# Two blocks of 384 tokens, not 256, in steps of seven products, with the outer products of the last 256 tokens put off to the end

## The chip, the core and the metric

The kernel runs on one core of one Trainium2 chip. The metric is the device time of one execution in microseconds. TensorE (PE) has a queue for its matmuls; its weight loads (PEld) overlap them. VectorE is DVE, ScalarE is ACT, GpSimd is POOL, and SP issues the DMAs. Every engine takes its instructions in the order in which the kernel wrote them.

## What is computed

```python
scores = scale * q @ k.T                      # B, H, S, D = 4, 8, 576, 64, causal
local = softmax(scores) @ v
q_p = phi(q)                                  # phi(x) = max(x, 0) + min(exp(x), 1)
mem_out = (q_p @ M_prev) / (q_p @ z_prev + 1e-6)
x = g * mem_out + (1 - g) * local             # as 2304 tokens x 512
out = ((x @ w_a) * (x @ w_b)) @ w_out         # 512 -> 1536 -> 512
```

## The kernel before

All large products are made of float32 operands split into a high and a low part (float32r), as three matmuls: high by high, low by high, high by low. The first 207 us are attention, with the results (`xo`) stored to DRAM (`xs`). Then comes the gated MLP on tokens as columns. The 1536 hidden features are 12 tiles `f` of 128.

**Columns.** Tokens are taken in blocks `t`: 0 to 3 of 384 tokens, 4 of 256. One pair (t, f) is called a column, and columns are numbered: block 2 is 24 to 35, block 3 is 36 to 47, block 4 is 48 to 59. A column is, on PE, 12 matmuls for `a` and 12 for `b` (`half`, L923, as wide as the block), and then the outer products of the column before it (`outer`, L961: 3 matmuls of 128x512 for each 128 tokens, which add into a PSUM bank each). Beside it ACT copies `b` (L936), DVE multiplies it by `a` (L939, "mx"), ACT rounds the result to the high part (L943) and DVE subtracts for the low part (`split_lo`, L201, tile `hl`). The third matmul of the outer products reads `hl`.

**Memory units.** The memory term of a block is made in units (block t, rows j) while PE works on earlier columns. `plan` says behind which column each part of a unit is written: on DVE `phi2`, `norm`, `norm2` (L1092 to L1126, the "first half"), then `norm3`, `turn`, `turn_l` (L1131 to L1137 and L201, the "turn", which waits in the middle for an ACT pass `yh`), then `join` (L1164); `sums` (L1147) on POOL adds the two halves of `xs` that `x_load` has fetched; `retrieve` (L1157) is PE's part.

**Steps.** The last 512 tokens, two blocks of 256, are taken together in 12 steps `step7(f)`. Sums and differences of the blocks (`combine`, L1192; `split_x`, L1205) and of the weight tile's quarters (`sums_load`, L1226, `sums_of` on POOL, L1236, `sums_split`, L1249 and L201) replace 8 half products by 7 (`part`, L1270, 6 matmuls each). Four products end in `h` (DVE L1309, L1310) and `u`; the outer products of a step (`out_rows`, L1342, 12 matmuls of 128x512) follow in the next step. PSUM has 8 banks: 4 hold the products (`ab`, `ab2`, two each), 4 the sums of the outer products (`o0` to `o2`, `m`). The bank of a step's first product is that of the step before, and is free once that step's `h` (L1310) has read it:

```python
        al = bank("ab")
        part(al, a11, B11, True)
```

The last 768 tokens thus take 24 + 42 matmuls of width 256 for each f, and 18 of width 512.

`ws` holds the weights of the 12 tiles as plain float32 in DRAM. `attention` opens PSUM pools `ps_t` (six banks) and `ps_w` (two, for the attention output `pw`), which are closed before `ab`, `o`, `o1` are opened over the same banks.

Of the kernel before, what the change touches and what calls it, by code (L numbers as in the profile page):

```python
# [136 lines left out]
def kernel(  # L137
# [37 lines left out]
    TH = 256  # L175
# [190 lines left out]
    def attention(late, early, tiles, after, more, beyond):  # L366
# [586 lines left out]
    def outer(t, f, h, ms=None):  # L953
        wh, wl = wt[f]
        w0 = 2 * KK * P
        for m in ms or range(WIDTH[t] // P):
            if f == 0:
                key = "o1" if t == 1 else "o"
                po[t, m] = pools[key].tile([P, DM], F32, tag=f"{key}{m}", name=f"{key}{m}")
            for n, (hx, w) in enumerate(((h[0], wh), (h[0], wl), (h[1], wh))):  # L960
                nc.tensor.matmul(  # L961
                    po[t, m], lhsT=hx[:, m * P:(m + 1) * P], rhs=w[:, w0:w0 + DM],
                    start=(f == 0 and n == 0), stop=(f == NFT - 1 and n == 2),
                )

    def written(t, m):
        if t == 2:
            ob = xf[0][:, (0, 3, 2)[m]].rearrange("p k c -> p (k c)")
        elif t == NB:
            ob = xf[0][:, m].rearrange("p k c -> p (k c)")  # L970
        elif t == 3:
            ob = pools["mem_b"].tile([P, DM], F32, tag=("q4", "ph", "q4")[m], name="ob", bufs=(2, 1, 2)[m])
# [7 lines left out]
        nc.sync.dma_start(out=out[r0:r0 + P, :], in_=ob)  # L980

# [6 lines left out]
    def hidden(c, n):  # L988
# [15 lines left out]
    def column(c, between):  # L1004
# [7 lines left out]
        if f == NFT - 1:  # L1012
            for m in range(WIDTH[t] // P):
# [10 lines left out]
    def memory_unit(pool, ps_m, t, j):  # L1024


        J = 1 if t < NB - 1 else 2
        js = slice(j, j + J)
        T0, TW = START[t], WIDTH[t]
# [37 lines left out]
        def x_load():  # L1067
            if J == 1:
# [7 lines left out]
            else:  # L1076
                x = xf[0][:, 3]
                if (t, j) == rest[-1]:
                    x = pool.tile([P, J, TW], F32, tag="q4", name="xx", bufs=2)
                r["x"] = xf[0][:, (1 + j + t - NB) % 4], x  # L1080
# [104 lines left out]
    PLACE = {B22: 0, B11: 1, T1: 1, TT2: 1, T4: 1, B12: 2, T3: 2, B21: 3}  # L1185
# [52 lines left out]
    def sums_split(f):  # L1238
# [4 lines left out]
        if f % 3 == 2:  # L1243
            two = [w[:, 0:3 * Q] for w in wt[0]]
        else:
            two = [pools["ring"].tile([P, 3 * Q], F32R, tag=f"s{f % 3}{n}", name="s" + n) for n in "hl"]
        ring[f] = two, [w[:, 2 * Q:3 * Q] for w in wt[f]]
# [4 lines left out]
    def step7(f):  # L1252
# [6 lines left out]
        a11, a12, a22 = (quarter(wt[f], i) for i in (0, 1, 3))  # L1259
# [33 lines left out]
        else:  # L1293
            split_x(T4, B22)
            sums_load(3)
# [7 lines left out]
        if f:  # L1303
            sums_split(f + 1)
            sums_load(f + 3)
# [7 lines left out]
        def hh(i, h):  # L1313
            two[i] = [pools["w2"].tile([P, TB], F32R, tag=nm, name=nm)[:, 0:TH] for nm in ("hh", "hl")]
            nc.scalar.activation(out=two[i][0], in_=h, func=AF.Copy)

        def hl(i, h):
            split_lo(nc.vector, two[i][1], h, two[i][0])

        hh(0, h1)  # L1320
        if f < NFT - 1:
            prev[4]()
        hl(0, h1)
        sums_of(f + 2)
        part(ga, s4, B22)
        if f == NFT - 1:
            prev[4]()
# [5 lines left out]
        def out_rows(i):  # L1333
            wh, wl = (w[:, 4 * Q:4 * Q + DM] for w in wt[f])
            for m in (2 * i, 2 * i + 1):
                if f == 0:
                    key, tag = (("o", "o2"), ("m", "m"), ("o", "o0"), ("o", "o1"))[m]
                    po[NB, m] = pools[key].tile([P, DM], F32, tag=tag, name=tag)
                a = (m - 2 * i) * P
                hi, lo = (x[:, a:a + P] for x in two[i])  # L1340
# [10 lines left out]
    def last_rows(m):  # L1351
        t, f = columns[-1]
        outer(t, f, cols[len(columns) - 1][1][1:], (m,))
        written(t, m)

    def arrange(c):
        at = c - 4 * NFT
        if at == 0:
            pieces()
            split_x(B11)  # L1360
        if at == 1:
            combine(T1)
            split_x(T1)
        if at == 2:
            combine(TT2)
            split_x(TT2)
        if at == 3:
            combine(T3)
        if at == 4:
            split_x(B21)  # L1370
            combine(T4)
        if at == 5:
            memb.close()
            md.close()
            for key, n in ("xe", 1), ("ring", 1), ("u", 1), ("ob", 2):
                pool(mlp_r, key, "right", n)
            xc[T3] = [
                pools["xe"].tile([P, 2, TH], F32R, name=f"xe{n}") for n in "hl"
            ]
            split_x(T3)  # L1380
            sums_load(0)
        if at == 6:
            sums_of(0)
        if at == 7:
            sums_split(0)
            sums_load(1)
        if at == 8:
            sums_of(1)
        if at == 9:
            sums_split(1)  # L1390
            sums_load(2)
# [3 lines left out]
    columns += [(t, f) for t in range(2, NB) for f in range(NFT)]  # L1395
# [8 lines left out]
    for j in range(KK):  # L1404
        c = 2 * NFT + (0, 3, 6, 8)[j]
        planned(3, j, (c - 1, False, 0, 2), (c, False, 2, 11), (c + 2, True, 11, 15))
    AT = range(36, 48, 2)
    rest = (4, 0), (4, 2), (5, 0), (6, 0), (6, 2), (5, 2)
    for n, (t, j) in enumerate(rest):
        c = AT[n]  # L1410
        for o, mid, what in (
            (-3 if n else -2, True, "load"), (-1 if n else 0, False, "phi phi2 norm norm2"),
            (0, False, "x_load"), (0, False, "norm3 turn turn_h turn_l"), (1, False, "sums"),
            (2, True, "retrieve join"), (2, False, "join_h join_l" if t < NB else ""),
        ):
            plan.setdefault((c + o, mid), []).extend((t, j, nm) for nm in what.split())

    def unit_step(t, j, nm):
# [5 lines left out]
        if nm == "load":  # L1424
            if t == NB - 1 and j == 0:
# [3 lines left out]
                xf[0] = pools["xf"].tile([P, 4, 2, TH], F32, name="xf")  # L1429
# [10 lines left out]
    with tc.manual_schedule():  # L1440
# [85 lines left out]
        last["h"] = None, None, None, lambda: last_rows(0), lambda: last_rows(1)  # L1526
        for f in range(NFT):
            step7(f)
        for go in last["h"]:
            go()  # L1530
# [32 lines left out]
```

## Time and profile before

| | us |
|---|---|
| median of 3 runs (665.22 to 666.14) | 665.34 |
| the profiled execution | 666.34 |
| its span, first to last instruction | 664.2 |
| PE busy in the span | 652.4 |
| DVE busy in the span | 499.0 |

The granted TensorE clock is full (1.00) from the start to 650 us, and 0.94 on average in the last 14 us. A matmul's time in the trace is longer than the distance to the next one, since matmuls are pipelined; what PE takes for one is therefore read from the starts of successive matmuls.

### The profile page before, as it was taken

Reading aid. Unit: us, or ns where it says so; the run is one execution under the profiler, and the core shown is the slowest. Engines: PE = TensorE matmul, PEld = TensorE weight load, DVE = VectorE, ACT = ScalarE, POOL = GpSimd, SP = SyncE. Lnnn points to the kernel's source line nnn. Section 1 sums busy time; section 2 is a strip of 40 time slices with the busy share of each in tenths; the row PEclk is TensorE's granted clock in tenths of the full one; section 3 lists DMA queues with packets and bytes.
Section 4 is the critical chain, followed back from the end, with each engine's and each line's share of the span. In section 5 each row is a group of like instructions: output and inputs, shape, how many; then the busy total and the mean of one; then the engine's idle time right before and its main releaser. Section 6 shows DMA issues by size and latency. Waiting matters only on the chain.

```text
span 664.2 us, 12217 instructions
## 1 busy us (share of the span) xinstructions
PE 652.4 (98%) x4338; PEld 600.9 (90%) x4338; DVE 499.0 (75%) x1012; ACT 333.2 (50%) x797; POOL 273.4 (41%) x400
## 2 busy tenths in 40 slices
PE   9899999999989999999999999999999999999997
PEld 7788899999978999999999999999999999999996
DVE  6999998888888887879898757458766433666664
ACT  6999999999885544544323222222222323332221
POOL 4999999999993222124102201000100012344410
PEclk9999999999999999999999999999999999999999
DMA  8965657466833444533345432133220111211101
GB/s 182 198 183 132 161 127 192 116 180 180 264 117 136 160 153 163 183 123 72 100 139 163 150 113 69 20 100 71 70 57 25 47 33 64 96 65 64 64 33 63
DMA packets 131259, 76.88 MB, mean 116 GB/s; under 512 B 98816, under 2 KB 118272, under 8 KB 131200
## 3 DMA queue, kind: packets, MB, share of 16 engines
q1 hardware_dynamic: 131200, 76.12, 40.6%
q8 instruction: 34, 0.56, 0.4%
q14 instruction: 25, 0.20, 0.1%
HBM read 55.64 MB, written 20.45 MB: 115 GB/s over the span
## 4 chain that ended last, share of the span: by engine, by line
PE 81%; DVE 8%; SPq 3%; ACT 3%; DMA 2%; POOL 1%; issue 1%; ACTq 0%; DVEq 0%; POOLq 0%
PE pp L923 32%; PE o L961 16%; PE pp L1270 9%; PE pt L197 6%; PE pw L711 5%; PE pt L545 4%; PE o L1342 4%; DVE PT L201 3%; DVE nm L584 2%; SPq L1053 2%; POOL P L611 1%; PE m L1157 1%; PE m L1342 1%; PE pw L545 1%; ACT P L594 1%; DMA qr<-in_q_dram 1%
## 5 line engine op out<-in xcount | busy, mean ns | idle before, releaser
L923 PE MATMUL pp<-xh,wh 128*128 128x384 f32 (+1 forms) x472 | 153.7, 326 | 1.5 <-ACT xo L720 0.8
L923 PE MATMUL pp<-xh,wl 128*128 128x384 f32 (+1 forms) x472 | 153.5, 325 | 0.0
L923 PE MATMUL pp<-xl,wh 128*128 128x384 f32 (+1 forms) x472 | 153.2, 325 | 0.0
L923 PEld LDWEIGHTS pp<-xh,wh 128*128 128x128 f32 x472 | 88.9, 188 | 4.5 <-ACT x L936 1.2
L923 PEld LDWEIGHTS pp<-xl,wh 128*128 128x128 f32 x472 | 88.9, 188 | 2.4
L923 PEld LDWEIGHTS pp<-xh,wl 128*128 128x128 f32 x472 | 88.9, 188 | 0.0
L611 POOL TENSOR_SCALAR P<-P,sum 128x384 f32<-128x384 f32 (+4 forms) x144 | 80.8, 582 | 4.9 <-DVE sum L603 4.5
L936 ACT ACTIVATE x<-pp 128x384 f32<-128x384 f32 (+1 forms) x59 | 27.5, 467 | 102.0 <-PE pp L923 86.7
L1236 POOL TENSOR_TENSOR xf<-xf 128x256 f32<-128x256 f32 x48 | 36.3, 757 | 99.7 <-DMA xf<-ws 55.3
L201 DVE TENSOR_TENSOR PT<-pt,PT 128x512 fp32r<-128x512 f32 (+2 forms) x112 | 62.7, 588 | 10.4 <-ACT PT L666 8.1
L594 ACT ACTIVATE P<-pt,nm 128x128 f32<-128x128 f32 (+3 forms) x128 | 66.8, 530 | 5.1 <-DVE nm L584 3.4
L939 DVE TENSOR_TENSOR x<-pp,x 128x384 f32<-128x384 f32 (+1 forms) x59 | 31.1, 527 | 48.2 <-ACT x L936 46.1
L961 PE MATMUL o<-wh,hl 128*128 128x512 f32 x168 | 66.3, 395 | 0.0
L961 PE MATMUL o<-wl,hh 128*128 128x512 f32 x168 | 66.3, 394 | 0.0
L961 PE MATMUL o<-wh,hh 128*128 128x512 f32 x168 | 66.2, 394 | 0.0
L711 PE MATMUL pw<-PT,vh 128*128 128x320 f32 (+4 forms) x416 | 63.0, 295 | 1.0 <-DVE PT L201 0.6
L711 PEld LDWEIGHTS pw<-PT,vh 128*128 128x128 f32 x416 | 57.6, 189 | 3.6 <-DVE PT L201 1.9
L584 DVE TENSOR_REDUCE nm<-pt 128x1 f32<-128x128 f32 (+3 forms) x128 | 55.8, 478 | 3.5 <-PE pt L545 3.2
L866 POOL TENSOR_SCALAR wt<-wt 128x512 f32<-128x512 f32 (+1 forms) x21 | 21.0, 1000 | 83.8 <-ACT wt L860 83.8
L197 PE MATMUL pt<-ident,P 128*128 128x128 f32 (+1 forms) x400 | 52.8, 276 | 2.5 <-POOL P L611 1.0
L666 ACT ACTIVATE PT<-pt 128x512 fp32r<-128x512 f32 (+2 forms) x112 | 52.6, 526 | 2.8 <-PE pw L711 1.7
L943 ACT ACTIVATE hh<-x 128x384 fp32r<-128x384 f32 (+1 forms) x60 | 30.1, 501 | 40.6 <-DVE x L939 31.2
(192 smaller groups left out, 1471.6 us busy)
## 6 DMA issues: line engine op xcount, KB each, us to landing
xs<-xo SPq DMA_DIRECT2D x16, 576.0 KB, 4.6
xx<-xs SPq DMA_DIRECT2D x32, 192.0 KB, 3.5
wr<-in_moe_w_a_dram SPq DMA_DIRECT2D x12, 512.0 KB, 3.7
wr<-in_moe_w_b_dram SPq DMA_DIRECT2D x12, 512.0 KB, 4.8
wr<-in_moe_w_out_dram SPq DMA_DIRECT2D x12, 512.0 KB, 5.7
ws<-fw SPq DMA_DIRECT2D x24, 256.0 KB, 2.5
xf<-ws SPq DMA_DIRECT2D x12, 512.0 KB, 3.2
qr<-in_q_dram SPq DMA_DIRECT2D x34, 128.0 KB, 3.2
```

Of the source, the lines that this page charges most:

```text
L197: nc.tensor.transpose(out, x, ident[0:x.shape[0], 0:x.shape[0]])
L201: eng.tensor_tensor(out=lo, in0=x, in1=hi, op=ALU.subtract)
L545: nc.tensor.matmul(o, lhsT=w, rhs=x, start=first, stop=True, skip_group_check=True)
L584: nc.vector.tensor_reduce(out=s["nm"][:, c:c + 1], in_=src, axis=AX.X, op=ALU.min)
L594: nc.scalar.activation(out=s["P", i][:, h, :], in_=src, func=AF.Exp, scale=-1.0, bias=s["nm"][:, c:c + 1], accum_out=s["sums"][:, c, 0:1],)
L611: nc.gpsimd.tensor_scalar(out=pr[:, h, :], in0=pr[:, h, :], scalar1=r[:, c:c + 1], scalar2=1.0, op0=ALU.mult, op1=ALU.mult,)
L666: nc.scalar.activation(out=dst, in_=src, func=AF.Copy)
L711: nc.tensor.matmul(pv[:, a:hi], lhsT=w, rhs=x, start=(n == 0), stop=(n == len(ops) - 1))
L923: nc.tensor.matmul(pp, lhsT=w[:, w0:w0 + P], rhs=x[:, kk, :], start=(c == 0), stop=(c == 3 * KK - 1),)
L961: nc.tensor.matmul(po[t, m], lhsT=hx[:, m * P:(m + 1) * P], rhs=w[:, w0:w0 + DM], start=(f == 0 and n == 0), stop=(f == NFT - 1 and n == 2),)
L1236: nc.gpsimd.tensor_tensor(out=o, in0=x, in1=y, op=op)
L1270: nc.tensor.matmul(o, lhsT=a[:, kk * P:(kk + 1) * P], rhs=b[:, kk, :], start=first and c == 0, stop=True, skip_group_check=True,)
```

## The change

Blocks 4 and 5 are now both 384 wide and go through `step7` together; block 4 as a block of columns of its own is gone. For each f the last 768 tokens take 42 matmuls of width 384. The outer products of those tokens need six banks of sums and only four are there, so those of the last 256 tokens are put off: `h` of these tokens is kept for all 12 tiles in SBUF (`kept`), and `end` computes their outer products behind step 11, one group of 512 columns and two of 256, in the banks that the products have left. To make room, block 3 takes its tiles in the order 9, 10, 11, 0 to 8, the weights of the three are given up, and `back` makes parts of them again from `ws` in steps 7 to 9. The quarter sums have one buffer for odd and one for even tiles in place of three; `sums_split(f + 1)` now stands in step 0 too. Eight memory units 384 wide (4 for each of blocks 4 and 5) replace six units of two row groups 256 wide, and `TURN` sets their places in half columns. `ps_w` is opened before `ps_t`.

```diff
-    START = [0, TB, 2 * TB, 3 * TB, 4 * TB, 4 * TB + TH, 4 * TB + 2 * TH]
-    WIDTH = [TB] * 4 + [TH] * 3
-    NB = 5
+    NB = 4
+    START = [t * TB for t in range(NB + 2)]
...
+        ps_w = late.enter_context(tc.tile_pool(name="ps_w", bufs=1, space=bass.MemoryType.PSUM))
         ps_t = late.enter_context(tc.tile_pool(name="ps_t", bufs=1, space=bass.MemoryType.PSUM))
-        ps_w = late.enter_context(tc.tile_pool(name="ps_w", bufs=1, space=bass.MemoryType.PSUM))
...
+    ORDER = {t: list(range(NFT)) for t in range(NB)}
+    away = range(NFT - 3, NFT)
+    ORDER[NB - 1] = [*away, *range(NFT - len(away))]
...
+    def back(f):
+        if f in away:
+            for c in slice(0, 2 * Q), slice(3 * Q, 4 * Q):
+                hi, lo = (w[:, c] for w in blocks_of(f))
+                nc.scalar.activation(out=hi, in_=ring[f][:, c], func=AF.Copy)
+                split_lo(nc.vector, lo, ring[f][:, c], hi)
+
+    def kept(f):
+        if f < len(away):
+            return [w[:, 3 * Q:4 * Q] for w in wt[away[f]]]
+        return [w[:, 0:Q] for w in blocks_of(f)]
...
-        if f % 3 == 2:
-            two = [w[:, 0:3 * Q] for w in wt[0]]
+        if f % 2 == 0:
+            two = [w[:, 0:3 * Q] for w in wt[away[0]]]
...
             split_x(T4, B22)
-            sums_load(3)
...
-        if f:
-            sums_split(f + 1)
-            sums_load(f + 3)
+        sums_split(f + 1)
+        if f == 0:
+            sums_load(2)
+        sums_load(f + 3)
...
+        for g in range(len(rest)):
+            late_rows(g, *range(NFT - 1))
+        second()
+        for g, (o, a, c0, n) in enumerate(rest):
+            late_rows(g, NFT - 1)
+            leave(o[:, 0:n], *OUT[4 + g], START[NB] + 4 * P + a, g % 2, c0)
...
-        if at == 9:
-            sums_split(1)
-            sums_load(2)
+        if at == 11:
             sums_split(0)
             sums_load(1)
             sums_of(1)
...
-    AT = range(36, 48, 2)
+    TURN = [50, 53, 61, 63, 70, 73, 75, 78, 80, 83, 85, 88]
```

DVE's queue late in block 3, before: the multiplications (L939) of columns 46 and 47 with what stands ahead of and between them. `m` and `xf` belong to a unit's `join`, `ph`, `q` and `yl` to its turn.

```order
L1164 TENSOR_TENSOR xf<-m,xf 128x512
L939 TENSOR_TENSOR x<-pp,x 128x384
L201 TENSOR_TENSOR hl<-x,hh 128x384
L1131 TENSOR_TENSOR ph<-ph,n_6644 128x512
L1137 STREAM_TRANSPOSE q_6479<-ph 128x512
L201 TENSOR_TENSOR yl<-q_6479,yh 128x512
L939 TENSOR_TENSOR x<-pp,x 128x384
```

The same queue after the change, from column 43's multiplication (L937 now) to that of column 44; the rows of width 768 are `split_x` and `combine`.

```order
L937 TENSOR_TENSOR x<-pp,x 128x384
L200 TENSOR_TENSOR hl<-x,hh 128x384
L200 TENSOR_TENSOR wl_4553<-xf,wh_4552 128x768
L1205 TENSOR_TENSOR xf<-xf 128x768
L1171 TENSOR_TENSOR xf<-m,xf 128x384
L1138 TENSOR_TENSOR ph<-ph,n_6569 128x384
L1144 STREAM_TRANSPOSE q_6479<-ph 128x384
L200 TENSOR_TENSOR yl<-q_6479,yh 128x384
L937 TENSOR_TENSOR x<-pp,x 128x384
```

The sums of blocks that stood in the columns of block 4 now stand between the units in block 3.

DVE's queue at the passage from the columns to step 0, before: the last column's multiplication, then step 0 down to its `h`.

```order
L939 TENSOR_TENSOR x<-pp,x 128x256
L201 TENSOR_TENSOR hl<-x,hh 128x256
L1290 TENSOR_TENSOR u_7318<-pp,x 128x256
L201 TENSOR_TENSOR xl_83<-xf,xh_82 128x512 x2
L1301 TENSOR_TENSOR u_7344<-pp,x 128x256
L1302 TENSOR_TENSOR u_7344<-u_7344,pp 128x256
L1309 TENSOR_TENSOR h_7359<-pp,x 128x256
L1310 TENSOR_TENSOR h_7359<-pp,h_7359 128x256
```

After the change, the same place (`wl_4521` and `wl_3642` are `sums_split(0)`, `sl` and `wl_3775`'s low part `sums_split(1)`):

```order
L200 TENSOR_TENSOR hl<-x,hh 128x384
L200 TENSOR_TENSOR wl_4521<-xf,wh_4520 128x768
L200 TENSOR_TENSOR wl_3642<-xf,wh_3641 128x256
L1319 TENSOR_TENSOR u_6858<-pp,x 128x384
L200 TENSOR_TENSOR xl_85<-xf,xh_84 128x768 x2
L1329 TENSOR_TENSOR u_6883<-pp,x 128x384
L1330 TENSOR_TENSOR u_6883<-u_6883,pp 128x384
L200 TENSOR_TENSOR sl<-xf,sh 128x768
L200 TENSOR_TENSOR wl_3776<-xf,wh_3775 128x256
L976 COPY xf<-o_6144 128x512
L1338 TENSOR_TENSOR h_6910<-pp,x 128x384
L1339 TENSOR_TENSOR h_6910<-pp,h_6910 128x384
```

Both splits of quarter sums, which stood behind columns 55 and 57 of 60, moved to the passage itself, the second in front of `h`.

## Rows read from the trace of the kernel before

**Rows 1.** Profile page, part 1: busy us (share of the span) xinstructions of each engine.
```profile
PE 652.4 (98%) x4338; PEld 600.9 (90%) x4338; DVE 499.0 (75%) x1012; ACT 333.2 (50%) x797; POOL 273.4 (41%) x400
```
**Rows 2.** Windows: stretch, length, busy us (instructions) by engine, clock, DMA share, GB/s.
```profile
325.00:350.00 25.00, 25.00 (x134) 23.36 (x133) 22.81 (x53) 7.50 (x16) 2.30 (x2) 1.00 0.51 138
450.00:475.00 25.00, 25.00 (x138) 23.34 (x137) 19.34 (x44) 7.30 (x14) 3.01 (x2) 1.00 0.33 71
575.00:600.00 25.00, 25.00 (x172) 23.14 (x171) 16.47 (x36) 6.45 (x16) 9.07 (x13) 1.00 0.19 64
```
**Rows 3.** Waits of PE, 150 to 664 us: total us, times, longest.
```profile
PE pp L923 <- ACT xo L720: 0.8, 1, 0.8
```
**Rows 4.** Timeline, PE: start us, us, engine, line, operation.
```profile
416.76 0.39 PE L961 MATMUL o<-wh,hh 128*128 128x512 f32 x1
...
423.59 0.39 PE L961 MATMUL o<-wh,hh 128*128 128x512 f32 x1
...
559.42 0.40 PE L961 MATMUL o<-wh,hh 128*128 128x512 f32 x1
...
563.69 0.40 PE L961 MATMUL o<-wh,hh 128*128 128x512 f32 x1
```
**Rows 5.** Chain that ended last, two steps: start us, us, what xcount.
```profile
577.53 1.39 PE o L1342 x6
...
585.31 1.40 PE o L1342 x6
```
**Rows 6.** Timeline, DVE, 332 to 447 us: parts of units, one column's pair.
```profile
332.06 0.56 DVE L1095 SCALAR_TENSOR_TENSOR ph<-q,ph 128x384 f32<-128x384 f32 x1
...
335.30 0.56 DVE L1131 TENSOR_TENSOR ph<-ph,n 128x384 f32<-128x384 f32 x1
...
338.04 0.35 DVE L1092 TENSOR_SCALAR ph<-ph 128x384 f32<-128x384 f32 x1
...
436.93 0.56 DVE L939 TENSOR_TENSOR x<-pp,x 128x384 f32<-128x384 f32 x1 [4.63 <-ACT x L936]
438.08 0.56 DVE L201 TENSOR_TENSOR hl<-x,hh 128x384 fp32r<-128x384 f32 x1 [0.59 <-ACT hh L943]
438.56 0.68 DVE L976 COPY xf<-o 128x512 f32<-128x512 f32 x1
...
444.12 0.69 DVE L1131 TENSOR_TENSOR ph<-ph,n 128x512 f32<-128x512 f32 x1
...
446.86 0.55 DVE L939 TENSOR_TENSOR x<-pp,x 128x384 f32<-128x384 f32 x1
```
**Rows 7.** Timeline, one quarter split and one set of quarter sums.
```profile
557.75 0.84 ACT L1249 ACTIVATE sh<-xf 128x768 fp32r<-128x768 f32 x1 [1.09 <-POOL xf L1236]
...
558.62 0.96 DVE L201 TENSOR_TENSOR sl<-xf,sh 128x768 fp32r<-128x768 f32 x1 [1.50 <-ACT sh L1249]
...
563.30 3.25 POOL L1236 TENSOR_TENSOR xf<-xf 128x256 f32<-128x256 f32 x4 [5.59 <-DMA xf<-ws]
```
**Rows 8.** Profile page, part 6: DMA xcount, KB each, us to landing.
```profile
xf<-ws SPq DMA_DIRECT2D x12, 512.0 KB, 3.2
```
**Rows 9.** Timeline: a POOL addition and the DVE instruction beside it.
```profile
492.46 1.29 POOL L1147 TENSOR_TENSOR xf<-xf 128x512 f32<-128x512 f32 x1 [12.12 <-DMA xf<-xs]
...
492.84 1.32 DVE L201 TENSOR_TENSOR hl<-x,hh 128x384 fp32r<-128x384 f32 x1 [0.59 <-ACT hh L943]
```
**Rows 10.** Groups by form, DVE, 420 to 664 us: xcount | busy us, mean ns.
```profile
L201 DVE TENSOR_TENSOR hl<-x,hh 128x384 fp32r<-128x384 f32 x15 | 9.8, 654 | 8.9 <-ACT hh L943 8.9
```
**Rows 11.** Timeline, 206 to 214 us, and the last copy.
```profile
206.21 0.74 ACT L720 ACTIVATE xo<-pw,ungate 128x576 f32<-128x576 f32 x1 [0.69 <-PE pw L711]
207.00 0.45 PE L923 MATMUL pp<-xh,wh 128*128 128x384 f32 x1 [0.83 <-ACT xo L720]
...
213.35 0.55 DVE L939 TENSOR_TENSOR x<-pp,x 128x384 f32<-128x384 f32 x1
...
660.51 0.69 DVE L976 COPY xf<-o 128x512 f32<-128x512 f32 x1 [0.70 <-PE o L1342]
```

More of the change, by code (lines that the diff above doesn't have):

```diff
@@ L962, in outer @@
                     po[t, m], lhsT=hx[:, m * P:(m + 1) * P], rhs=w[:, w0:w0 + DM],
-                    start=(f == 0 and n == 0), stop=(f == NFT - 1 and n == 2),
+                    start=(f == ORDER[t][0] and n == 0), stop=(f == ORDER[t][-1] and n == 2),
                 )
+    OUT = [(k * DM, DM) for k in (2, 3, 0, 1, 4)] + [(5 * DM, DM // 2), (5 * DM + DM // 2, DM // 2)]
     def written(t, m):
[L967 to L972, printed above, removed]
+        if t == NB:
+            leave(po[t, m], *OUT[m], START[t] + m * P, m % 2)
+            return
+        if t == 2 or t == 3 and m < 2:
+            a = m if t == 2 else 3 - m
+            ob = xf[0][:, a * DM:(a + 1) * DM]
         else:
@@ L1011, in column @@
         t, f = columns[c - 1]
-        if f == NFT - 1:
-            for m in range(WIDTH[t] // P):
+        if f == ORDER[t][-1]:
+            for m in range(TPB):
                 written(t, m)
@@ L1076, in x_load @@
             else:
[L1077 to L1080, printed above, removed]
+                a = j % 2
+                x = pool.tile([P, J, TW], F32, tag="xx", name="xx")
+                r["x"] = place(RAW[t - NB][j // 2])[:, a:a + 1, :], x
                 for h, n in ((h, n) for h in range(2) for n in range(2)):
@@ L1349, in step7, with last_rows, end, late_rows @@
         last["h"] = (both, lambda: hh(1, u3), lambda: hl(1, u3), lambda: out_rows(0), lambda: out_rows(1))
-    def last_rows(m):
+    def last_rows(*ms):
         t, f = columns[-1]
-        outer(t, f, cols[len(columns) - 1][1][1:], (m,))
-        written(t, m)
+        for m in ms:
+            outer(t, f, cols[len(columns) - 1][1][1:], (m,))
+            written(t, m)
+    def end():
+        both, hh, hl, first, second = last["h"]
+        both()
+        hh()
+        hl()
+        first()
+        rest = [(pools[k].tile([P, DM], F32, tag="ab", name="pr"), a, c0, n) for k, a, c0, n in (
+            ("ab", 0, 0, DM), ("ab2", P, 0, DM // 2), ("ab2", P, DM // 2, DM // 2),
+        )]
+        def late_rows(g, *fs):
+            o, a, c0, n = rest[g]
+            for f in fs:
+                wh, wl = (w[:, 4 * Q + c0:4 * Q + c0 + n] for w in wt[f])
+                hi, lo = (x[:, a:a + P] for x in kept(f))
+                for i, (hx, w) in enumerate(((hi, wh), (hi, wl), (lo, wh))):
+                    nc.tensor.matmul(
+                        o[:, 0:n], lhsT=hx, rhs=w,
+                        start=(f == 0 and i == 0), stop=(f == NFT - 1 and i == 2),
+                    )
+        for g in range(len(rest)):
[4 more added lines that the diff above has]
+            leave(o[:, 0:n], *OUT[4 + g], START[NB] + 4 * P + a, g % 2, c0)
@@ L1370, in arrange @@
             split_x(B21)
             combine(T4)
[L1372 to L1380, printed above, removed]
             sums_load(0)
-        if at == 6:
+        if at == 10:
             sums_of(0)
-        if at == 7:
+        if at == 11:
@@ L1525 @@
             arrange(c)
-        last["h"] = None, None, None, lambda: last_rows(0), lambda: last_rows(1)
+        last["h"] = None, None, None, lambda: last_rows(0, 1), lambda: last_rows(2)
         for f in range(NFT):
             step7(f)
-        for go in last["h"]:
-            go()
+        end()
         mlp_r.close()
```

135 lines of the change are left out of this document (78 added, 57 removed).

## The prediction, made before the changed kernel ran

> **What bounds the kernel now.** I read the busy times first: PE is busy for 652.4 of 664.2 us, DVE for 499 [rows 1]. An average over stages says little, so I took windows next: from 325 to 600 us PE has no gap in the trace, while DVE falls from 22.81 busy us in 25 (units of block 3 beside other work) to 19.34 in block 3 and 16.47 in the steps [rows 2]. The waits of PE show only short ones, of which one matters here: 0.8 us for the copy `xo` at the start of the MLP [rows 3]. So PE's own work sets the end over the whole stretch that the change touches, and the question is whether DVE, which it loads more densely, still keeps ahead.
>
> **PE's work.** I take what a matmul costs from distances between starts. Column to column in block 2 it is 423.59 - 416.76 = 6.83 us for 9 matmuls of width 512 and 27 of 384 (three belong to a `retrieve`) [rows 4]. Six of width 512 take 1.40 [rows 5], 0.233 each, so one of 384 takes (6.83 - 2.10) / 27 = 0.175. A column of block 4 takes 563.69 - 559.42 = 4.27 [rows 4], so one of 256 takes (4.27 - 1.40) / 24 = 0.12. A step takes 585.31 - 577.53 = 7.78 [rows 5]. Per f, before: 4.27 + 7.78 = 12.05. After: 42 x 0.175 + 12 x 0.233 = 10.15 for a step, and 3 x 0.233 + 6 x 0.12 = 1.42 for the outer products put off, 11.57. That saves 0.48 x 12 = 5.8. The `retrieve`s lose 24 matmuls of 256 and gain 12 of 384 (24 narrow ones stay 24), another 24 x 0.12 - 12 x 0.175 = 0.8. **PE: -6.6 us.** If 384 goes at 0.174, which other columns' spacing allows, it is -7.1.
>
> **DVE in block 3.** What was spread over the columns of blocks 3 and 4 now stands in block 3: eight units, `combine` and `split_x` of width 768. I added up DVE's queue, from Z, the end of column 36's products, to the low part `hl` of column 43. Prices: a column's pair 438.56 - 436.93 = 1.63, ACT pass included; a unit's first half 335.30 - 332.06 = 3.24 and 0.39 for its opening pass of 0.35; a turn 446.86 - 444.12 = 2.74 at width 512, for 384 about 2.25 (four passes shorter by some 0.13 each); a `join` about 0.48 (like "mx", 0.56, less what overlaps) [rows 6]; a 768-wide pass 0.96, and 0.84 on ACT ahead of a split [rows 7]. The queue starts at Z + 2.9, since its first `join` waits for the `retrieve` behind 9 outer matmuls. It holds 6 joins (2.9), 6 turns (13.5), 6 first halves (21.8), 7 pairs (11.4), 4 wide passes (3.8) with 1.3 of waits for ACT: 54.7, so it ends at Z + 57.6. PE wants that `hl` after 8 columns (8 x 6.3 = 50.4), seven `retrieve`s (3 x 0.72 + 4 x 0.525 = 4.3) and two matmuls (0.5): Z + 55.2. DVE is 2.4 late.
>
> Beside it POOL adds six times (`sums`). One such addition stands against a DVE pass of 1.32 in place of 0.56, 0.76 lost [rows 9]; over the 15 `hl` passes the mean is 0.654 [rows 10], 1.4 us too much in a stretch with six additions, 0.23 each. I take that: 1.4. PE waits on `hl` in its outer products, with the next column's products behind them: **+3.8 us**, between 1.2 (every DVE price 3% less) and 7 (each addition costs 0.76). Afterwards DVE has little to do until column 47, so nothing of it is carried into the steps.
>
> The Trainium skill ("SBUF — State Buffer", section "Who interferes with whom") says that VectorE and GpSimd share one port pair as an exclusive lock: the loser waits for the whole instruction. The row with 1.32 agrees. By the rule six additions of about 1.0 (an estimate: the 1.29 of rows 9, scaled from 512 to 384 elements) could cost DVE 5.8 in place of 1.4, and the sum would come to 669.1; by the mean of the group it is what stands in the sum.
>
> **Passage to the steps.** `sums_load(1)` writes where tile 0's sums lie, so it waits for `sums_split(0)`, which now follows column 47; and `sums_split(1)` stands in DVE's queue ahead of the `h` that frees the bank for step 1's first product. From Y, the end of column 47's products: ACT copy 0.6, "mx" and the high part 438.08 - 436.93 = 1.15 [rows 6]; ACT 0.84, DVE 0.96 [rows 7] and some 0.4 for its 256-wide part; DMA 3.2 [rows 8]; POOL 3.25; again 0.84, 0.96 and 0.4 [rows 7]; a copy of outer sums 0.68, two passes for `h` 1.12 [rows 6]. Sum 14.4. PE until step 1: 2.1 for column 46, 7.35 + 2.1 in step 0, 11.55. **+2.8 us**, between 2 and 3.5 with the load and POOL a little faster or slower. Before, the second split was long done when step 0 began. From step 1 on a step is 10.15 long; DVE has 8 passes of 0.56, splits of 1.4 and waits for ACT, `back` adds 1.1 in three steps: some 7.5, below PE. One buffer each for odd and even tiles suffices, as tile f + 1's sums are written when step f - 1 has ended. I price these edits at nothing; uncovered, `back` would cost 3 x 1.1.
>
> **Banks.** With `ps_w` below, the first MLP product no longer takes the bank that `xo` is read from: 0.83 of idle goes [rows 11]. But the product after next waits for "mx" at 213.35 [rows 11], which hangs on weight conversion; PE reaches it at about 214.26 today (207.00, 24 products, the wait at 212.17, 12 more), when 213.9 would do. I take **-0.3**, between -0.8 and 0.
>
> **End.** The kept products run behind step 11 while DVE and ACT make that step's last `h`, so they wait for nothing. The last copy is 256 wide and on ACT, about 0.4 in place of 0.69 [rows 11]: **-0.3**, between -0.6 and 0.
>
> **Sum.** -6.6 + 3.8 + 2.8 - 0.3 - 0.3 = -0.6. The profiled execution took 666.34 (span 664.2 and 2.1 around it), the median is 665.34; I take the difference off the median: **664.7 us**. About 0.2%, 1.3 us, is what a measurement can tell from no change.
>
> **Rivals.** *DVE keeps up.* In 325 to 350 us DVE was 91% busy and PE idle for nothing [rows 2]; if its queue in block 3 runs some 4% faster than I added it up, or the passes overlap more, only the passage costs: -6.6 + 2.8 - 0.6 = -4.4, 660.9; without that stall too, 658.1. Against it: the queue is longer than PE's stretch by my prices, and each pair's wait for ACT stands in it. Chance 0.2.
>
> *POOL's additions cost DVE more.* With DVE without a gap, each addition must meet a DVE pass; at 0.76 each [rows 9] six cost 4.6, not 1.4: +3.2 on the forecast, 667.9. It decides from 0.6 each on, where the sum passes +1.3 us. Against it: the mean over many passes [rows 10]. Chance 0.2.
>
> *The narrower gain.* If a 384-wide matmul in the steps took 0.187, PE would save nothing there; block 2's spacing speaks against it. This, and a wait that I have not seen (queries landing late for a unit, whose ACT pass stands ahead of a column's copy), are the remaining 0.05, slower.
>
> **Chances.** The forecast, with 4.5 to 8.5 us of new waits, has 0.55 and reaches from -2.9 to +1.1 us (662.4 to 666.4); of it 0.18 lies under -1.3 and 0.35 between -1.3 and +1.3, 0.02 above. With the rivals: faster 0.18 + 0.2 = 0.38, slower 0.02 + 0.17 of the second rival + 0.05 = 0.24, the same 0.35 + 0.03 = 0.38. For the range I leave out the half of the first rival with no wait in the passage, and what lies above the second with a little for its spread: 661 to 668.5.
>
> **What would show it.** Right: steps 1 to 11 at 10.1 us; no DVE gap worth the name between 440 and 500 us, with PE waiting for `hl` in columns 39 to 44, most in 43; one PE wait for `h` between steps 0 and 1 of 2 to 3 us; no wait for `xo` near 207 us. Wrong: PE without waits in block 3, or `h` early in step 0 because tile 1's sums came sooner; or PE waits in later steps, which would mean that one buffer of quarter sums or `back` is on the path.

## The result, and the profile after

| | before | after |
|---|---|---|
| median on one chip, us | 665.43 (665.22 to 666.14, 4 runs) | 670.34 (669.41 to 671.89, 4 runs) |
| ratio, 95% interval | | 1.0068 [1.0056, 1.0081] |
| the profiled execution, us | 666.34 | 671.89 |

The change costs 4.9 us, where the prediction had -0.6 and a range up to 668.5. I read the trace in the order of the prediction. First the page's part 1 and the windows, which answer to [rows 1, 2]:

```profile
PE 651.3 (97%) x4074; PEld 598.7 (89%) x4074; DVE 516.4 (77%) x1030; ACT 332.4 (50%) x794; POOL 277.2 (41%) x402
```

Windows of the kernel after: stretch, length, busy us of PE, PEld, DVE, ACT, POOL, granted clock, DMA share, GB/s.

```profile
450.00:475.00 25.00, 23.99 (x124) 21.51 (x123) 19.97 (x50) 6.40 (x14) 3.55 (x3) 1.00 0.27 59
475.00:500.00 25.00, 22.39 (x109) 19.40 (x108) 20.63 (x45) 5.77 (x13) 3.55 (x3) 0.94 0.21 54
500.00:525.00 25.00, 25.00 (x135) 23.39 (x134) 12.33 (x19) 8.66 (x16) 3.72 (x6) 0.99 0.14 43
525.00:550.00 25.00, 21.57 (x103) 20.46 (x102) 14.59 (x25) 7.23 (x16) 11.84 (x15) 0.86 0.29 94
550.00:575.00 25.00, 25.00 (x132) 23.35 (x132) 16.93 (x31) 5.64 (x13) 6.45 (x8) 1.00 0.17 52
```

PE, which had no gap from 325 to 600 us, now idles in three of these stretches, and the clock, which stood at 1.00 there, falls to 0.94 and 0.86. PE's waits from 440 us to the end, in total, times and longest:

```profile
PE pp L1299 <- DVE h L1339: 3.4, 1, 3.4
PE o L959 <- ACT hh L941: 3.3, 2, 2.2
PE m L1164 <- ACT yh L1148: 0.2, 1, 0.2
```

The two places are the ones that were forecast: the passage, with `h` of step 0 (3.4 us, forecast 2.8), and block 3, with the high part `hh` of columns 39 and 43 (1.01 and 2.25; the forecast has `hl`, one DVE pass later, and 3.8 in all). The chain of work that ended last shows the passage to the steps as the prediction wrote it: split of tile 0's sums, load, four additions on POOL, split of tile 1's sums, and only then `h`, which frees the bank.

```profile
519.46 1.30 DVE wl L200 x2
...
520.82 3.19 DMA xf<-ws
...
524.15 0.74 POOL xf L1265
...
527.36 0.85 ACT sh L1278
...
529.57 0.94 DVE wl L200
530.51 0.60 DVE xf L976
...
531.61 0.57 DVE h L1339
...
532.22 7.90 PE pp L1299 x29
```

What the prediction had no term for stands behind the waits. PE's timeline, at the end of step 0 and in step 1:

```profile
528.29 0.33 PE L1299 MATMUL pp<-xl,wh 128*128 128x384 f32 x1
528.46 0.34 PE L1299 MATMUL pp<-xh,wl 128*128 128x384 f32 x1
532.22 0.69 PE L1299 MATMUL pp<-xh,wh 128*128 128x384 f32 x1 [3.42 <-DVE h L1339]
532.71 0.52 PE L1299 MATMUL pp<-xl,wh 128*128 128x384 f32 x1
533.03 0.52 PE L1299 MATMUL pp<-xh,wl 128*128 128x384 f32 x1
...
538.04 0.34 PE L1299 MATMUL pp<-xeh,wh 128*128 128x384 f32 x1
```

Ahead of the wait a matmul starts 0.17 us after the one before; behind it 0.32. The 18 matmuls from 532.22 to 538.04 took 5.82 us, where 18 at 0.175 take 3.15: 2.7 us lost. The granted clock in that stretch is 0.50, the lower of the two levels (1.2 GHz, not 2.4). Behind the wait of 2.25 us the same:

```profile
495.40 0.50 PE L959 MATMUL o<-wh,hh 128*128 128x512 f32 x1 [2.25 <-ACT hh L941]
...
496.98 0.63 PE L959 MATMUL o<-wh,hl 128*128 128x512 f32 x1
...
498.68 0.52 PE L921 MATMUL pp<-xh,wh 128*128 128x384 f32 x1
...
500.50 0.34 PE L921 MATMUL pp<-xh,wh 128*128 128x384 f32 x1
```

Four of width 512 in 1.70 us and six of 384 in 1.82, where 0.93 and 1.05 would do: 1.5 us lost. The Trainium skill ("TensorE: Matmul & The Clock Gate", section "HAM oscillation — how this bites in real kernels") describes a wait for data, there a DMA's, that sends the next tile off at the lower clock; these rows agree in kind.

### The profile page after: what moved, and what is told of

It is laid out like the page before. It is cut to its first block, busy times and chain, and to the rows that moved or that the text cites. A ratio compares the mean times of both kernels' runs of the same rounds, so it can differ in the third digit from the quotient of the medians.

```text
span 670.1 us, 11702 instructions
## 1 busy us (share of the span) xinstructions
PE 651.3 (97%) x4074; PEld 598.7 (89%) x4074; DVE 516.4 (77%) x1030; ACT 332.4 (50%) x794; POOL 277.2 (41%) x402
## 4 chain that ended last, share of the span: by engine, by line
PE 72%; DVE 17%; DMA 3%; ACT 2%; issue 2%; SPq 2%; POOL 1%; DVEq 0%; ACTq 0%; POOLq 0%
PE pp L921 24%; PE pp L1299 12%; PE o L959 12%; PE pt L196 5%; PE pw L710 4%; DVE PT L200 4%; PE pt L544 4%; PE o L1375 4%; DVE nm L583 3%; PE pr L1406 3%; PE m L1375 1%; PE pw L544 1%; DMA qr<-in_q_dram 1%; PE m L1164 1%; DVE wl L200 1%
## 5 line engine op out<-in xcount | busy, mean ns | idle before, releaser
L921 PE MATMUL pp<-xh,wh 128*128 128x384 f32 x376 | 126.9, 337 | 0.9 <-ACT x L934 0.9
L921 PE MATMUL pp<-xh,wl 128*128 128x384 f32 x376 | 126.5, 337 | 0.3 <-DVE wl L200 0.3
L921 PE MATMUL pp<-xl,wh 128*128 128x384 f32 x376 | 126.3, 336 | 0.0
L921 PEld LDWEIGHTS pp<-xh,wh 128*128 128x128 f32 x376 | 70.9, 189 | 3.4 <-ACT x L934 1.9
L921 PEld LDWEIGHTS pp<-xl,wh 128*128 128x128 f32 x376 | 70.9, 189 | 1.6
L921 PEld LDWEIGHTS pp<-xh,wl 128*128 128x128 f32 x376 | 70.8, 188 | 0.6 <-DVE wl L200 0.6
L200 DVE TENSOR_TENSOR PT<-pt,PT 128x512 fp32r<-128x512 f32 (+2 forms) x112 | 62.7, 588 | 10.4 <-ACT PT L665 8.1
L959 PE MATMUL o<-wl,hh 128*128 128x512 f32 x144 | 57.0, 396 | 0.0
L941 ACT ACTIVATE hh<-x 128x384 fp32r<-128x384 f32 x48 | 25.0, 522 | 55.4 <-DVE x L937 45.9
L934 ACT ACTIVATE x<-pp 128x384 f32<-128x384 f32 x47 | 22.8, 486 | 53.5 <-PE pp L921 37.5
L196 PEld LDWEIGHTS pt<-ident,P 128*128 128x128 f32 (+1 forms) x400 | 44.1, 140 | 5.8 <-POOL P L610 2.5
```

Source lines behind the costliest of these rows:

```text
L196: nc.tensor.transpose(out, x, ident[0:x.shape[0], 0:x.shape[0]])
L200: eng.tensor_tensor(out=lo, in0=x, in1=hi, op=ALU.subtract)
L921: nc.tensor.matmul(pp, lhsT=w[:, w0:w0 + P], rhs=x[:, kk, :], start=(c == 0), stop=(c == 3 * KK - 1),)
L959: nc.tensor.matmul(po[t, m], lhsT=hx[:, m * P:(m + 1) * P], rhs=w[:, w0:w0 + DM], start=(f == ORDER[t][0] and n == 0), stop=(f == ORDER[t] ...
```

## The experiments

All are the changed kernel with one edit, except where said. Each ran on one chip beside the kernel before, whose median there was 665.9 to 666.1; so ratios are compared, and 0.001 is 0.67 us. The changed kernel itself has 1.0068.

| kernel | median us | ratio to before, 95% interval |
|---|---|---|
| split behind `h` | 665.87 | 0.9996 [0.9987, 1.0005] |
| filled wait | 669.05 | 1.0048 [1.0035, 1.0060] |
| ten units earlier | 677.12 | 1.0170 [1.0156, 1.0184] |
| both of these (first and third) | 672.13 | 1.0096 [1.0082, 1.0110] |
| banks alone, in the kernel before | 665.97 | 1.0001 [0.9992, 1.0009] |
| eight units two earlier | 672.30 | 1.0099 [1.0083, 1.0114] |
| tile 0's split a column earlier | 667.21 | 1.0021 [1.0009, 1.0033] |
| units and block 3's end earlier | 666.93 | 1.0008 [0.9998, 1.0018] |
| units spread from 67 | 672.72 | 1.0100 [1.0085, 1.0115] |
| spread, split behind `h` | 668.26 | 1.0032 [1.0020, 1.0043] |
| spread, `u` first | 666.41 | 1.0004 [0.9996, 1.0013] |
| end earlier, spread from 66 | 664.94 | 0.9991 [0.9973, 1.0008] |
| passage alone | 664.36 | 0.9977 [0.9968, 0.9987] |
| block 3 alone | 666.55 | 1.0004 [0.9993, 1.0015] |
| both repairs | 661.00 | 0.9924 [0.9912, 0.9936] |

**Split behind `h`.**

```diff
-        sums_split(f + 1)
+        if f:
+            sums_split(f + 1)
...
         nc.vector.tensor_tensor(out=h1, in0=al, in1=h1, op=ALU.mult)
+        if f == 0:
+            sums_split(1)
+            sums_load(3)
```

> The split of tile 1's sums stands behind step 0's `h` in the queues of DVE and ACT, not ahead of it; nothing else changes. After the change PE was idle for 3.42 us ahead of step 1, and the 18 matmuls behind that wait took 5.82 us where 18 at 0.175 take 3.15, at a granted clock of 0.50: 2.7 lost. Theory (the wait is the split ahead of `h`, and the fall of the clock belongs to the wait): both go, 670.3 - 3.4 - 2.7 = 664.2 us, granted clock 1.00 from 525 to 550 us. Rival A (the clock falls there whatever PE waits for): only the wait goes, 666.9. Rival B (tile 1's split itself comes too late, whatever stands behind it): the wait moves to step 1's second product and stays above 1 us, 668 or more.

The ratio fell by 0.0072, 4.8 us. The window from 525 to 550 us, and PE's wait in it:

```profile
525.00:550.00 25.00, 23.69 (x126) 21.99 (x125) 18.90 (x31) 7.85 (x17) 12.69 (x16) 1.00 0.32 100
...
532.42 0.41 PE L1299 MATMUL pp<-xh,wh 128*128 128x384 f32 x1 [1.31 <-DVE u L1368]
```

The clock was 1.00. PE waited 1.31 us, for the sum `u` that frees another bank and now stood behind the split: the shortfall of the theory's 6.1.

**Filled wait.** The same products as step 1's first one, three times, into a bank that is started anew afterwards.

```diff
+        if f == 1:
+            be = bank("ab2")
+            for _ in range(3):
+                part(be, a11, B11, True)
         al = bank("ab")
         part(al, a11, B11, True)
...
-        be = bank("ab2")
+        if f != 1:
+            be = bank("ab2")
```

> The changed kernel, with 18 matmuls of width 384 put into PE's queue ahead of step 1's first product. They write a bank whose next true product starts it anew, so the output is the same; they take about 3.15 us at full clock, of the 3.42 in which PE has been idle, and step 1 still has to wait for `h`. Theory (PE's idle brings the clock down): the clock stays at 1.00 from 525 to 550 us and the 2.7 us lost behind the wait come back, 667.6 us, though PE does more work. Rival A (the clock falls whatever PE does there, or its loss lies in the wait itself): no gain, 670.3 or up to 3 us more if the added matmuls run at half clock.

Windows of 2 us, of this kernel:

```profile
530.00:532.00 2.00, 2.00 (x14) 2.00 (x13) 2.00 (x3) 0.11 (x1) 1.88 (x2) 1.00 0.00 0
532.00:534.00 2.00, 1.65 (x9) 1.33 (x9) 1.37 (x4) 0.65 (x2) 0.25 (x1) 1.00 0.74 156
534.00:536.00 2.00, 2.00 (x13) 2.00 (x13) 1.65 (x4) 1.29 (x4) 0.23 (x1) 1.00 0.92 326
```

and of the changed kernel:

```profile
530.00:532.00 2.00, 0.00 (x0) 0.00 (x0) 1.97 (x4) 0.00 (x0) 1.01 (x2) 0.77 0.27 45
532.00:534.00 2.00, 1.78 (x6) 1.78 (x7) 1.38 (x4) 1.01 (x2) 0.00 (x0) 0.50 0.94 260
534.00:536.00 2.00, 2.00 (x8) 2.00 (x8) 0.37 (x1) 1.39 (x4) 1.24 (x2) 0.50 0.91 348
```

Step 1 began as long after step 0 as before, but with PE at work (0.35 us of idle left) the clock stayed at 1.00, and with 18 matmuls more the median ratio is 0.0020 lower, 1.3 us. The two intervals just touch, and this is one trace, so what carries the reading is the clock: in all five traces in which PE stood 3.4 to 3.5 us ahead of step 1 (the changed kernel, ten units earlier, eight units two earlier, units spread, block 3 alone) it was 0.50 behind that wait, and PE lost 1.6 to 3.0 us there. So the loss behind the wait belongs to PE's idling. That only half of 2.7 came back is not settled; in this profiled execution PE stood 1.1 us later already at step 0, with a wait of 0.7 for `hl` in block 3 that the changed kernel's trace does not have.

**Ten units earlier,** and **both of these.**

```diff
-    TURN = [50, 53, 61, 63, 70, 73, 75, 78, 80, 83, 85, 88]
+    TURN = [50, 53, 55, 58, 63, 66, 69, 72, 75, 78, 81, 85]
```

> Only the table of the memory units' places changes: ten of the twelve units stand 2 to 7 half columns earlier, where DVE was busy 17 to 18 of 25 us. The additions on POOL are as many, and as many of them stand beside DVE. Theory (DVE's queue in block 3 is too long, 1.01 + 2.25 us of PE idle, 0.6 in the matmuls just behind the two waits and 1.5 of half clock behind the second): all go, 670.3 - 5.4 = 664.9 us, clock 1.00 from 450 to 525 us. Rival (what POOL's additions cost DVE makes the waits, not the queue's length): they stay within 1 us of what they were, 669 or more.

> The split behind `h` and the earlier units together. Theory: the two gains add up, 670.3 - 6.1 - 5.4 = 658.8 us, PE without a wait over 0.3 us from 210 us to the end, and the granted clock full; that is 6.6 under the kernel before, what PE's work was to save. Rival A (the clock falls anyway): the waits alone go, 663. Rival C (PE's matmuls save less than 6.6 us, so that the loss has another part): 660 to 662 with no wait left.

Both theories missed on the sum. PE's waits of the first, by the timeline:

```profile
400.70 0.69 PE L1164 MATMUL m<-yh,md 128*128 128x384 f32 x1 [5.61 <-ACT yh L1148]
410.20 0.44 PE L1164 MATMUL m<-yh,md 128*128 128x384 f32 x1 [1.81 <-ACT yh L1148]
...
537.05 0.69 PE L1299 MATMUL pp<-xh,wh 128*128 128x384 f32 x1 [3.47 <-DVE h L1339]
```

From 450 to 525 us the waits are gone, but block 3's own units now met the sums of weights (`weight_whole`) on DVE, and lost more at 395 us. The two edits add up: the second kernel is 0.0074 under the first, as the split behind `h` alone gave 0.0072.

**Banks alone,** in the kernel before.

```diff
+        ps_w = late.enter_context(tc.tile_pool(name="ps_w", bufs=1, space=bass.MemoryType.PSUM))
         ps_t = late.enter_context(tc.tile_pool(name="ps_t", bufs=1, space=bass.MemoryType.PSUM))
-        ps_w = late.enter_context(tc.tile_pool(name="ps_w", bufs=1, space=bass.MemoryType.PSUM))
```

> The kernel before, with the pool of two banks opened ahead of the pool of six, and nothing else. The prediction took -0.3 us for it; the trace of the changed kernel shows 0.35 us less of PE idle from 200 to 225 us, but its columns near 300 us stand only 0.13 us earlier. Expected -0.1 to -0.35 us, too little to be told from no change; a rival: 0.8 us, the whole of the wait for the copy.

No difference that can be told; the interval excludes 0.8 us.

**Eight units two half columns earlier.**

```diff
+    TURN = [50, 53, 61, 63, 68, 71, 73, 76, 78, 81, 83, 86]
```

> The changed kernel; only the eight units of the last two blocks stand two half columns earlier, those of block 3 where they were. In the wider shift of the run with ten earlier units the waits of 450 to 525 us were gone, and a new one of 5.6 us stood at 395 us, where block 3's units met the stores of the weights. Theory (DVE's queue starts too late for its length; two half columns are some 6.5 us): the waits in block 3 go with what follows them, 1.0 + 2.25 + 0.6 + 1.5, so -5.4 against the changed kernel, 0.5 us under the kernel before; clock 1.00 from 450 to 525 us; no wait near 395 us. Rival (the load of the queue in 425 to 450 us is enough to push the waits there): less than half of it.

The theory fell: the waits of block 3 moved earlier and grew, to 4.8 us.

```profile
451.61 0.50 PE L959 MATMUL o<-wh,hh 128*128 128x512 f32 x1 [0.86 <-ACT hh L941]
...
456.88 0.44 PE L1164 MATMUL m<-yl,md 128*128 128x384 f32 x1 [0.51 <-DVE yl L200]
...
461.36 0.50 PE L959 MATMUL o<-wh,hh 128*128 128x512 f32 x1 [1.77 <-ACT hh L941]
...
490.77 0.50 PE L959 MATMUL o<-wh,hh 128*128 128x512 f32 x1 [1.65 <-ACT hh L941]
```

Eight units in eighteen half columns are as dense wherever they begin.

**Tile 0's split a column earlier,** and **units and block 3's end earlier.**

```diff
         if at == 10:
             sums_of(0)
-        if at == 11:
             sums_split(0)
             sums_load(1)
             sums_of(1)
```

> The changed kernel with the split of tile 0's sums, the load of tile 1 and its additions one column earlier in the queues. POOL ends tile 0's additions only at 516.8 us, so the chain gains some 2.1 us, not a column of 6.3, and the last column's copy on ACT waits about 1 us behind the split, which nothing on PE needs. Theory: the wait ahead of step 1 falls from 3.4 to about 1.3 us, and since the wait of 1.01 us in block 3 was not followed by half clock, the 2.7 us behind it go too: -4.8 against the changed kernel, about the time of the kernel before. Rival (half clock follows any wait there): -2.1, still 2.8 over the kernel before.

The second has the units of the run before and `at == 8`, `9`, `10` for `9`, `10`, `11` at the three places of `arrange`.

> The units two half columns earlier, and with them the whole end of block 3 (last sums of blocks, loads, additions and splits of tiles 0 and 1) one column earlier, so that tile 1's sums are ready before step 0's `h`. Theory: no wait of PE over 0.3 us from 450 us on and full clock: what PE's work saves is left, -6.6 and the small terms, 658 to 659 us where the kernel before takes 665.4. Rival C (PE's work saves less than 6.6 us): 660 to 662 with no wait left. Rival D (the passage's wait comes from something else than the lateness of tile 1's sums): a wait of over 1 us stays ahead of step 1, 662 or more.

In the first the wait for `h` was 2.4 us, not 1.3, without half clock in the profiled execution; the gain is 0.0047, 3.1 us. Its twelve executions are one program, and their times go by the mean granted clock:

| mean granted clock | executions | us |
|---|---|---|
| 1.000 | 5 | 665.74 to 666.80 |
| 0.997 | 4 | 667.12 to 667.55 |
| 0.995 | 3 | 668.60 to 669.57 |

Its profiled execution is one of the first row. Its wait in block 3 is 2.23 us, that of the changed kernel 2.25, and here nothing follows:

```profile
494.00:496.00 2.00, 0.76 (x3) 0.34 (x3) 1.36 (x4) 1.26 (x2) 1.00 (x1) 1.00 0.00 0
496.00:498.00 2.00, 2.00 (x9) 1.68 (x10) 2.00 (x3) 0.00 (x0) 0.00 (x0) 1.00 0.03 8
498.00:500.00 2.00, 2.00 (x14) 2.00 (x13) 1.29 (x3) 0.56 (x2) 0.00 (x0) 1.00 0.00 0
```

where the changed kernel had 0.73 and 0.50 in the last two stretches. So half clock follows a wait of this length in some executions and not in others. In the second kernel no wait was left in the passage, but 4.9 us in block 3, with half clock behind the longest (2.59): 666.9, not 658 to 662.

**Units spread,** alone, with the split behind `h`, and with `u` first.

```diff
+    TURN = [50, 53, 60, 62, 67, 70, 73, 76, 79, 82, 85, 88]
```

> The changed kernel; the eight units of the last two blocks stand three half columns apart, from 67 to 88, in place of eighteen half columns from 70 to 88, and two of block 3's stand one earlier. Theory (what counts is how densely the units stand: 8 units at 6.4 us of DVE, ten pairs and the sums of blocks need some 68 us, eighteen half columns last about 59, twenty-one about 69; a shift as a whole, which was tried, changes nothing): the waits in block 3 fall from 3.3 us to under 1 us, with no half clock behind them; the wait ahead of step 1 stays at 3.4. So -3 to -5.4 against the changed kernel, 665 to 667.5 us. Rival (any place that is earlier pushes the waits earlier, as in the shift by two): waits of 3 us or more between 430 and 500 us, 669 or more.

> The spread units, and the split of tile 1's sums behind step 0's `h`. Of the passage a wait of about 1.3 us for `u` should be left, as in the run with that edit alone, and the clock full. Theory: PE's work, reckoned again from the traces (6.1 us less in the steps and block 4, next to nothing in the retrieves, the banks and the end), leaves -6.3, plus 1.3 and up to 1 of waits: 4 to 5 us under the kernel before, 661 to 662 us. Rival (PE's work is only some 4 us less, and the clock's loss larger than it seemed): 663 or more with no further wait.

```diff
         nc.vector.tensor_tensor(out=h1, in0=al, in1=h1, op=ALU.mult)
+        if f == 0:
+            sums_split(1, 0)
...
         part(ga, s4, B22)
+        if f == 0:
+            nc.vector.tensor_tensor(out=u2, in0=ga, in1=u2, op=ALU.add)
+            sums_split(1, 1)
+            sums_load(3)
+            hl(0, h1)
```

Here `sums_split(1, 0)` is the part 768 wide, the first three quarters, and `sums_split(1, 1)` the last quarter.

> As the run before it in this list, and in step 0 DVE makes the first part of the split, then the sum `u` that frees the bank, then the rest. The wait of 1.3 us should fall to 0.5 or less: about 0.8 us under the run with the spread units and the split behind `h`, 660 to 661 us. Rival (POOL's additions beside the split, 1.42 us in place of 0.96, hold DVE up as before): no difference from that run.

All three missed what was expected: 672.7, 668.3 and 666.4 us, where 665 to 667.5, 661 to 662 and 660 to 661 stood, with 4.7, 4.9 and 5.6 us of waits between 400 and 440 us. PE's waits in the first:

```profile
408.55 0.80 PE L959 MATMUL o<-wh,hh 128*128 128x512 f32 x1 [3.87 <-ACT hh L941]
437.36 0.50 PE L959 MATMUL o<-wh,hh 128*128 128x512 f32 x1 [0.82 <-ACT hh L941]
532.60 0.69 PE L1299 MATMUL pp<-xh,wh 128*128 128x384 f32 x1 [3.49 <-DVE h L1339]
```

Again nothing from 450 to 525 us and a new wait ahead of it: with block 3's fourth unit one half column earlier, its first half came ahead of a column's multiplication and not behind it. While PE stands there, DVE catches up, so this run does not show that density was the cause. The edit with `u` first left no wait from 500 us on, and is 0.0028 (1.9 us, where 0.8 was expected) under the kernel with the split behind `h`.

**End earlier, spread from 66.** The end of block 3 as above, and:

```diff
+    TURN = [50, 53, 59, 61, 66, 69, 72, 75, 78, 81, 83, 86]
```

> The end of block 3 one column earlier, as in the run that had it with the units two half columns earlier, where no wait was left in the passage; the units now stand three half columns apart from 66 to 81 and end at 86, so the last part of the queue is as dense as it was. Theory (density): the waits in block 3, 4.9 us there, fall to 1 to 2.5 us, the clock is full, 661 to 663 us. Rival (as many waits as with the units two earlier): 666 to 667.

3.9 us of waits were left, 2.0 of it in block 3, as the theory had it, and the rest at 400 us, where the theory had none; the time, 664.9, is not to be told from the kernel before.

**Passage alone, block 3 alone, both repairs.** The passage's repair is the one with `u` first. Block 3's leaves the first four units alone, moves six of the others one half column earlier and takes two sums of blocks out of the dense stretch:

```diff
+    TURN = [50, 53, 61, 63, 69, 72, 74, 77, 79, 82, 85, 88]
...
-        if at == 6:
-            combine(TT2)
         if at == 7:
-            split_x(TT2)
-            combine(T3)
+            combine(TT2)
+            split_x(TT2)
         if at == 8:
+            combine(T3)
             split_x(T3)
```

> The changed kernel with the passage's repair alone: in step 0 DVE makes `h`, the first part of tile 1's split, the first sum of `u`, then the rest. With the spread units this left no wait from 525 us on. Theory: the wait of 3.4 us and the half clock behind it go, the waits in block 3 (1.0 and 2.25 us, half clock behind the second in some executions) stay: about 665 us, 5 to 6 us under the changed kernel and within 1.5 us of the kernel before. Rival (most of the loss sits in block 3): 667 or more.

> Block 3's repair alone. Block 3's own units stay; six of the last two blocks' units stand one half column earlier; two sums of blocks move one column later, where DVE has time again. The shift by two half columns and the spread to 67 moved the waits rather than ending them, as PE's own waiting gave DVE time. Theory (3.3 us must be taken out of DVE's queue ahead of the products of columns 40 to 44, and here some 4 us are): waits in block 3 under 1.2 us in all, none elsewhere before step 0, the passage's 3.4 us left: 666.5 to 668.5 us. Rival (DVE is the bound from 400 to 500 us whatever the order): waits of 3 us or more from 400 to 500 us, 670 or more.

> Both repairs in one kernel. Theory: the two gains add up, no more than 1.2 us of waits from 400 us to the end and the clock full: PE's work of -6.3 us against the kernel before plus the waits, 660 to 661.5 us. Rival (DVE is the bound from 400 to 500 us): 663 or more.

The passage alone gained 0.0091 (6.1 us), block 3 alone 0.0064 (4.3), both 0.0144 (9.6); alone they would add up to 10.4. Block 3 alone still had 2.0 us of waits from 440 to 480 us, where under 1.2 was expected, and none of them had half clock behind it. PE's waits from 200 us on, with both:

```profile
PE o L959 <- ACT hh L941: 1.3, 1, 1.3
PE pp L921 <- ACT x L934: 0.8, 1, 0.8
PE o L959 <- ACT xf L978: 0.6, 1, 0.6
PE pp L921 <- DVE wl L200: 0.3, 1, 0.3
```

1.9 us from 400 us on, where 1.2 was expected. This kernel is 5.1 us faster than the one before: DVE can nearly keep up, and most of the loss was in the order of its queue.

## Why the prediction was wrong

**The step that failed** is the pricing of the two waits in the sum: "+3.8 us" for block 3 and "+2.8 us" for the passage are the times in which PE stands, and nothing was added for what PE does next. The rows of before show a granted clock of 1.00 in stretches from 325 to 600 us [rows 2], but also no gap of PE there (0.1 us in the whole trace from 325 to 600), so they held no evidence that it would stay so once PE waited. After the change 1.5 and 2.7 us were lost at 0.50, 4.2 in the profiled execution. The filled wait and the five traces with a wait of 3.4 us show that it goes with PE's idling. The profiled execution is the slowest of four, with the lowest mean clock (0.992; the others, 669.4 to 670.8 us, have 0.995 to 0.997), so 4.2 is the upper end of what the clock took.

**The balance** of the profiled execution, by the prediction's terms: PE -6.6, as forecast; block 3 1.01 + 2.25 + 0.2 of waits, and 1.4 in the matmuls at and just behind them, which start later than their spacing, 4.9 in all (forecast 3.8); passage 3.6 from start to start (2.8); banks -0.2, as the columns from 280 to 430 us stand 0.13 to 0.18 us earlier (-0.3); end -0.1, from the last matmul's start to the end of the span (-0.3); half clock 4.2, for which the forecast had no term. Sum +5.8, where the two spans differ by 5.9 and the two profiled executions by 5.5. Without the last term it is +1.6: 2.2 over the forecast of -0.6, and inside its range.

**PE's work** was right as far as the traces go: `h` of step 2 stands at 553.46 and that of step 11 at 644.83, nine steps of 10.15 each, as forecast. With both repairs the kernel gains 5.1 us in spite of 1.9 of waits.

**Block 3.** The place was right (columns 39 to 44, most in 43), and the size 1.1 us too small. PE's own stretch was right: 55.3 us without the waits, 55.2 forecast. One term of DVE's queue was too small: POOL's additions. DVE's timeline shows passes that met one, and the same pass without:

```profile
443.90 1.49 DVE L1125 COPY n<-n 32x12 f32<-32x12 f32 x4
...
454.25 0.70 DVE L1125 COPY n<-n 32x12 f32<-32x12 f32 x4
...
478.05 1.30 DVE L1138 TENSOR_TENSOR ph<-ph,n 128x384 f32<-128x384 f32 x1
...
481.10 0.35 DVE L1099 TENSOR_SCALAR ph<-ph 128x384 f32<-128x384 f32 x1
...
489.89 1.18 DVE L1099 TENSOR_SCALAR ph<-ph 128x384 f32<-128x384 f32 x1
```

Seven additions of 1.0 to 1.5 us between 444 and 496 us lengthened DVE's passes by 0.79, 0.55, 0.36, 0, 0.75 (against 0.55), 0.83 and 0.16, 3.4 us in all, 0.49 each, where the prediction took 0.23 and 1.4 in all. That is between the forecast and the rival (0.76), and close to 0.6, from which the rival decided. Yet the queue, from the first join at 438.98 to the end of column 43's `hl` at 496.10, took 57.1 us where 56.1 stood: its other prices were 1.0 us too high. That 3.8 came as near as it did is in part luck, two errors of opposite sign. The rule of the Trainium skill that the prediction cites ("SBUF — State Buffer", section "Who interferes with whom") gives an exclusive lock; that a whole addition is lost each time, as the prediction's sum by it has it, does not follow. The trace agrees with the lock: each of the six passes lost 0.1 to 0.2 us less than what was left of the addition when the two met (the pass at 489.89 lost 0.83 where 0.96 was left), and one addition, at 466.71 us, lengthened none.

**Passage.** Right in mechanism and place, and 0.6 us too small by the wait alone. POOL again took more than that: the split's passes took 1.41 and 0.94 us on DVE (0.96 and 0.4 forecast) beside tile 2's additions, 1.0 more, so the other terms were some 0.4 too high. From step 1 on there was no wait: `back` and the single buffers are hidden, as priced.

**The rival "DVE keeps up"** was wrong for this order and right in principle, as the kernel with both repairs shows. Shifting eight units by two half columns moved the waits; the repair of block 3 cut them from 3.5 to 2.0 us. It makes two edits at once, units earlier and sums later, and which of them did it was not tried. That what decides is which of DVE's passes stand between two multiplications fits these runs, but no run tests it by itself. Why 1.3 us is left there was not tried.

**Slips in the working.** With 4.5 to 8.5 us of new waits the terms reach from -2.7 to +1.3 us, not from -2.9 to +1.1, and for the first rival DVE's queue must run some 6% faster than added up, not 4%, as POOL's 1.4 us stands in it too. Neither decides the outcome.

## What to carry to other kernels

A new wait on an engine that never waited is not priced by its length alone: here 3.4 us of waiting brought 1.6 to 3.0 us more at half clock in each of five traces, and 2.2 us brought some 1.5 us in three of five and nothing in the others, so give it both ends in the range. When work is packed into fewer columns, add up the in-order engine's queue between each two passes that PE wants, and after a repair look for the wait ahead of the old place as well, since a wait there lets the queue catch up and hides the old one. In a queue, a long pass for the next step belongs behind the short one that frees a bank: that order alone, with the half clock that went with it, was worth 6.1 us.

## What the runs showed of the hardware

The clock after a wait differs between executions, of one program too. The trace of the changed kernel has 0.50 behind a wait of 2.25 us; that with tile 0's split a column earlier has 1.00 behind one of 2.23 us at the same place, and over its twelve executions the time runs from 665.7 to 669.6 us, with a mean clock from 1.000 to 0.995. The traces at the two places, by the wait that PE had:

| PE's wait, us | traces | with 0.50 behind it |
|---|---|---|
| 1.25 to 1.31, ahead of step 1 | 3 | 0 |
| 2.42, ahead of step 1 | 1 | 0 |
| 3.39 to 3.49, ahead of step 1 | 5 | 5 |
| 2.22 to 2.25, column 43 | 5 | 3 |

The length of a wait alone does not decide it: with the end of block 3 earlier and the units spread from 66, one of 1.44 us at 400 us has 0.50 behind it. The Trainium skill ("TensorE: Matmul & The Clock Gate", section "Part 1: The HAM clock gate (the "warmup" mystery)") says, of a kernel's start, that the number of slow matmuls varies from run to run of one kernel; these executions show a like spread behind a wait. What decides it in one execution no run here shows.
